# A fixed instruction order on every engine, 1024-column score steps, one-bank slots and a centred v, in a fused hash-attention and channel-mix kernel

## The chip, the cores and the metric

The kernel runs on one core of one Trainium2 chip. The metric is device time in microseconds of one execution. Most executions of one kernel agree closely; this kernel before the change spreads more than others (353 to 368 us in three runs). A run is called slow when it is over 1.5% above the fastest of the same kernel, and ratios below use fast runs alone. The profile of the kernel before fell in a slow run (366.5 us).

## The reference

Four batches, eight heads, 768 positions, head size 64. Each query attends only to keys in the same hash bucket; the result goes through a token-shifted channel mix.

```python
q_bits = (einsum('bhsd,dk->bhsk', q, proj) > 0)      # 6 bits; same for k
mask   = q_bucket[:, :, :, None] == k_bucket[:, :, None, :]
scores = where(mask, q @ k.T / 8, -1e9)
attn   = exp(scores - max);  attn /= attn.sum(-1) + 1e-9
x      = (attn @ v).transpose(0, 2, 1, 3).reshape(4, 768, 512)
x_prev = x shifted by one position, first row 0
xk = mu_k * x + (1 - mu_k) * x_prev                  # xr likewise with mu_r
out = sigmoid(xr @ w_r) * ((relu(xk @ w_k) ** 2) @ w_v)
```

A query whose bucket holds no key has to get the mean of v. The kernel does this with an epsilon weight on every key.

## The kernel before

It works on 16 pairs of heads. Four short names are used below. To "turn" is to transpose; q and k are first split into a rounded half (hi) and the remainder (lo). "Bit rows" are the six hash bits of each position, written by DMA as six more rows under q and k, so that the score matmul itself favours keys of the same bucket. "PV" is the product of the weights with v. A "mixed pair" is one beside which channel mix of an earlier batch runs. The parts that matter here:

```python
ps = ctx.enter_context(tc.tile_pool(name="ps", bufs=4, space=bass.MemoryType.PSUM))
# every use of PSUM takes one of these four slots of two banks, tag "s"

def mk_t(side):                  # split into hi and lo halves, turn by DMA
    ...                          # hi on POOL from pair 2 on, lo on VectorE
    nc.sync.dma_start_transpose(out=tr, in_=hl.rearrange("p c e -> p (c e)"))

def u_bits():                    # signs of the projections -> 6 bit rows under q and k
    bp = ps.tile([P, 2, 512], FP32, name=f"bp{n}", tag="s")
    ...                          # 16 matmuls, two VectorE passes
    nc.sync.dma_start(out=s["qk"[g // 2]][D:AUG, g % 2, :], in_=bt[G * g : G * g + NB, :])

def score_units(n):              # 12 units: 2 matmuls of 384 columns, one exp of 768
    ...
def pv_units(n):                 # epsilon: a matmul of eps_mat with the sum of v starts oo
    if ic == 0:
        hold["oo"] = ps.tile([P, 2, 512], FP32, name=f"oo{n}", tag="s")
        nc.tensor.matmul(hold["oo"][...], eps_mat, s["sv"]..., start=True, stop=False)
    ...                          # 72 matmuls of 65 columns into the slot; reciprocal; multiply

def k2_units(b):                 # relu on VectorE, square on POOL
    nc.vector.tensor_scalar(out=kr, in0=kp[:, :, 0:STRIP], scalar1=0.0, ..., op0=ALU.max)
    nc.gpsimd.tensor_tensor(out=k2, in0=kr, in1=kr, op=ALU.mult)

for n in range(NPAIRS):
    load(n + 3)
    ...
    weave(score_units(n + 1), front_units(n + 2), pv, moe.get(n, []))
```

The source order is not the order in which engines run: a scheduler may move an instruction ahead of others on its engine.

The softmax here doesn't subtract the row's maximum and nothing guards it: scores larger than these inputs give would overflow.

## Time and profile before

| | before |
|---|---|
| time, median of 3 runs | 358.08 us (353.14 to 367.58) |
| profiled execution | span 364.7 us, slow |
| first exp | 44.5 us |
| pairs 2 to 4, without channel mix | about 17 us each |
| end of the last exp to the end | 47.2 us (317.5 to 364.7) |

First the head of the profile page: the span, then busy time of each engine with its share. Below it are rows of the second part, 40 equal slices of the span (one is 9.1 us), with the busy share in tenths and the granted clock of TensorE in tenths of full speed.

```profile
span 364.7 us, 6121 instructions
PE 277.4 (76%) x2446; PEld 157.9 (43%) x2465; DVE 171.3 (47%) x275; ACT 176.1 (48%) x217; POOL 131.0 (36%) x187
...
PE   0020498396969698697979996969899989989795
...
ACT  1000197264746558275566683745567657710111
...
PEclk9999999556565699898999998978999999999989
DMA  7999789783735536456282560440616000011012
```

No engine is full on average. TensorE comes nearest and does next to nothing in the first four slices; after the eighth its row swings between 5 and 9. In slices 8 to 14 (63 to 126 us) the recorded clock is about half.

The waits view (engine, instruction, what it waited for, total us, times, longest):

```profile
ACT pt_242 L275 <- PE sc_0_0_243 L268: 42.2, 1, 42.2
...
PE bp_164 L213 <- DMA qt_157<-qhl_154: 19.9, 1, 19.9
...
PE sc_1_3_444 L268 <- DVE ob_462 L331: 6.0, 1, 6.0
```

The first says that no exp could start for 42 us. The second is why: the DMA transpose of q for pair 0 landed only at 19.9 us. The third is a score unit that waited 6 us for a PSUM slot that a normalisation had not yet read.

The stretch table (start and end in us, length, then busy us with instruction count for TensorE, its weight loads, VectorE, ScalarE and POOL, then granted clock, DMA share, GB/s):

```profile
75.00:92.00 17.00, 13.80 (x129) 8.30 (x127) 7.63 (x13) 10.50 (x13) 4.78 (x10) 0.60 0.66 170
...
285.00:300.00 15.00, 13.54 (x154) 8.51 (x152) 9.09 (x16) 9.96 (x13) 8.48 (x12) 1.00 0.02 4
```

The first is a pair without channel mix at half clock, the second one with mix at full clock. The chain of waits (start, length, what) leads in the tail through POOL's squares, one behind the other; TensorE has other matmuls beside most of them, and its own waits for squares come to 2.0 us there:

```profile
335.08 1.47 POOL k_3_0_3930 L388
336.55 1.43 POOL k_3_1_3943 L388
337.97 1.42 POOL k_3_2_3956 L388
```

### The profile page before, as it was taken

What the parts mean: (1) busy time and instruction counts of PE and PEld (TensorE: products, weight loads), DVE (VectorE), ACT (ScalarE), POOL (GpSimd) and SP (SyncE); (2) the same over time, 40 slices, a digit from 0 to 9 for tenths busy, and PEclk for the clock granted to TensorE, in tenths of its full rate; (3) what the DMA queues carried; (4) which work ended last, traced back from release to release, by engine and by line L of the source; (5) the groups of instructions that cost most, each with busy time, mean ns of one, the idle gap of its engine ahead of it and who ended that gap; (6) DMA issues with size and microseconds to landing.
All of it is one profiled execution on the core that took longest, in us unless ns stands there. A gap on an engine that the chain in (4) does not pass through costs nothing. (4 is left out here: it accounts for less than half of the span.)

```text
span 364.7 us, 6121 instructions
## 1 busy us (share of the span) xinstructions
PE 277.4 (76%) x2446; PEld 157.9 (43%) x2465; DVE 171.3 (47%) x275; ACT 176.1 (48%) x217; POOL 131.0 (36%) x187
## 2 busy tenths in 40 slices
PE   0020498396969698697979996969899989989795
PEld 0000245163636365363545552634455656555342
DVE  3321511636262566663545765633435665357422
ACT  1000197264746558275566683745567657710111
POOL 3643311522232356562323674622023642002900
PEclk9999999556565699898999998978999999999989
DMA  7999789783735536456282560440616000011012
GB/s 215 246 177 190 157 204 189 260 218 97 171 82 140 111 110 115 106 76 174 62 242 67 133 135 0 105 59 34 144 36 118 4 3 33 29 70 50 0 63 109
DMA packets 69788, 41.36 MB, mean 113 GB/s; under 512 B 51960, under 2 KB 66176, under 8 KB 69760
## 3 DMA queue, kind: packets, MB, share of 16 engines
q1 hardware_dynamic: 67632, 38.36, 44.1%
q0 software_dynamic: 2128, 2.62, 4.9%
q8 instruction: 19, 0.31, 0.4%
q14 instruction: 9, 0.07, 0.1%
HBM read 24.12 MB, written 6.29 MB: 83 GB/s over the span
## 5 line engine op out<-in xcount | busy, mean ns | idle before, releaser
L376 PEld LDWEIGHTS <-wk_sb 128*128 128x128 bf16 x256 | 25.3, 101 | 26.6 <-issue 13.0
L213 PEld LDWEIGHTS <-phi 128*32 128x32 f16 x128 | 4.3, 105 | 43.8 <-issue 36.9
L275 ACT ACTIVATE pt_242<-sc_0_0_243,exp_bias 128x768 bf16<-128x768 f32 x1 | 0.9, 902 | 42.2 <-PE sc_0_0_243 L268 42.2
L213 PE MATMUL bp_164<-qt_157,phi 128*32 128x384 f16 x4 | 1.0, 508 | 19.9 <-DMA qt_157<-qhl_154 19.9
L213 PE MATMUL bp_206<-qt_199,phi 128*32 128x384 f16 x4 | 1.0, 508 | 10.0 <-DMA qt_199<-qhl_196 10.0
L408 ACT ACTIVATE rs_0_4028<-vr_0_4023 128x512 f32<-128x512 f32 x1 | 0.6, 597 | 14.0 <-PE vr_0_4023 L400 14.0
L268 PEld LDWEIGHTS <-kt_162 70*128 70x128 f16 x24 | 3.3, 143 | 7.3 <-issue 4.1
L314 PEld LDWEIGHTS <-pt_694 128*128 128x128 bf16 x72 | 5.3, 137 | 2.4 <-issue 2.4
L314 PEld LDWEIGHTS <-pt_495 128*128 128x128 bf16 x72 | 5.2, 136 | 2.4 <-issue 2.4
L314 PEld LDWEIGHTS <-pt_242 128*128 128x128 bf16 x72 | 5.2, 134 | 2.4 <-issue 2.0
L314 PEld LDWEIGHTS <-pt_298 128*128 128x128 bf16 x72 | 5.1, 133 | 2.4 <-issue 2.4
L268 PEld LDWEIGHTS <-kt_204 70*128 70x128 f16 x24 | 2.4, 131 | 8.1 <-DVE ob_462 L331 6.4
L301 PEld LDWEIGHTS <-eps_mat 128*128 128x128 bf16 x32 | 3.4, 111 | 5.0 <-issue 3.4
L314 PE MATMUL oo_303<-va_188,pt_242 128*128 128x65 bf16 x72 | 5.5, 244 | 0.0
L314 PE MATMUL oo_897<-va_649,pt_694 128*128 128x65 bf16 x72 | 5.4, 246 | 0.0
L268 PE MATMUL sc_1_3_444<-qt_199,kt_204 70*128 70x384 f16 x2 | 0.8, 514 | 6.0 <-DVE ob_462 L331 6.0
L134 POOL TENSOR_SCALAR wv_sb<-wv_sb 128x2048 bf16<-128x2048 bf16 x2 | 3.9, 1948 | 4.0 <-DMA wv_sb<-in_moe_w_v_dram 4.0
L314 PE MATMUL oo_699<-va_452,pt_495 128*128 128x65 bf16 x72 | 5.3, 245 | 0.0
L314 PE MATMUL oo_500<-va_230,pt_298 128*128 128x65 bf16 x72 | 5.2, 241 | 0.0
L213 PE MATMUL bp_164<-kt_162,phi 128*32 128x384 f16 x4 | 1.1, 507 | 5.1 <-DMA kt_162<-khl_159 5.1
L213 PEld LDWEIGHTS <-plo 128*32 128x32 f16 x128 | 4.1, 109 | 1.5 <-issue 0.6
L240 POOL CAST va_3273<-vn_2807 128x768 bf16<-128x768 f32 x1 | 0.9, 896 | 10.8 <-PE oo_2835 L314 10.8
(1441 smaller groups left out, 996.5 us busy)
## 6 DMA issues: line engine op xcount, KB each, us to landing
wk_sb<-in_moe_w_k_dram POOLq DMA_DIRECT2D x2, 512.0 KB, 9.9
wv_sb<-in_moe_w_v_dram POOLq DMA_DIRECT2D x2, 512.0 KB, 12.4
wr_sb<-in_moe_w_r_dram POOLq DMA_DIRECT2D x1, 512.0 KB, 11.6
qn_134<-in_q_dram SPq DMA_DIRECT2D x1, 384.0 KB
kn_135<-in_k_dram SPq DMA_DIRECT2D x1, 384.0 KB
vn_136<-in_v_dram SPq DMA_DIRECT2D x1, 384.0 KB
qn_140<-in_q_dram SPq DMA_DIRECT2D x1, 384.0 KB
kn_141<-in_k_dram SPq DMA_DIRECT2D x1, 384.0 KB
```

Of the source, the lines that this page charges most:

```text
L134: nc.gpsimd.tensor_scalar(out=d, in0=d, scalar1=scale, scalar2=1.0, op0=ALU.mult, op1=ALU.mult)
L213: nc.tensor.matmul(bp[G * g : G * (g + 1), sp, 0:STRIP], (phi, plo)[w], s["qk"[g // 2]][:, g % 2, sp * STRIP : (sp + 1) * STRIP], start=(w ...
L240: nc.gpsimd.tensor_copy(va[:, :, :, 0:D], vn)
L268: nc.tensor.matmul(sc[:, sp, 0:STRIP], s["k"][0:AUG, j, jc * P : (jc + 1) * P], s["q"][0:AUG, j, sp * STRIP : (sp + 1) * STRIP], start=Tru ...
L275: nc.scalar.activation(pt[:, j, jc, :].rearrange("p (s q) -> p s q", s=2), sc[:, :, 0:STRIP], AF.Exp, bias=exp_bias, scale=EXP_SCALE,)
L301: nc.tensor.matmul(hold["oo"][:, j, 0 : NSC * W].rearrange("p (c w) -> p c w", c=NSC), eps_mat, s["sv"][:, j : j + 1, :].to_broadcast([P, ...
L314: nc.tensor.matmul(oo[:, j, ic * W : (ic + 1) * W], s["pt"][:, j, jc, ic * P : (ic + 1) * P], s["va"][:, j, jc, :], start=False, stop=(ic ...
L376: nc.tensor.matmul(kp[:, sp, 0:STRIP], wk_sb[:, dc, fc * P : (fc + 1) * P], mixed[b * NPB + dc][0][:, sp * STRIP : (sp + 1) * STRIP], star ...
L408: nc.scalar.activation(rs, vr[:, 1, :], AF.Tanh, scale=0.5)
```

## The change

The intent is to let TensorE run without gaps. Every engine gets a written order (a chain of dependencies without semaphores keeps each instruction behind the one before it in the source); each pair is nine steps of 1024 score columns with named side work at each step; the channel mix is dealt out evenly; PSUM is cut into two 2-bank slots for scores and four 1-bank slots for all else. Relu goes to ScalarE, squares and hi parts to VectorE. Pair 0 is turned by TensorE. The epsilon matmul is replaced: v has its mean taken off, the sum gets a plain epsilon, and the mean is added after the turn. Buffer counts change too (20 square buffers in place of 10, for strips half as long), and the loads are spread over the steps. The diff, cut to its core:

```diff
-    ps = ctx.enter_context(tc.tile_pool(name="ps", bufs=4, space=bass.MemoryType.PSUM))
+    sps = ctx.enter_context(tc.tile_pool(name="sps", bufs=2, space=bass.MemoryType.PSUM))
+    ops = ctx.enter_context(tc.tile_pool(name="ops", bufs=4, space=bass.MemoryType.PSUM))
+    def bank(name, shape=None, dtype=FP32):
+        return ops.tile(shape or [P, BANK], dtype, name=name, tag="o")
 ... (cut: loads, splits, turns)
+    def turn_by_pe(n, side):          # pair 0 only: 12 transposes, one copy out of PSUM
 ...
+    def v_mean(n):
+        nc.tensor.matmul(mp[:, 0:P], ones_mat, s["sv"], start=True, stop=True)
+        nc.tensor.matmul(mp[:, P : P + 1], s["sv"], ones_mat[:, 0:1], start=True, stop=True)
+        ...                           # va = v - mean, on POOL
 ...
-                nc.vector.tensor_scalar(out=kr, ..., op0=ALU.max)
-                nc.gpsimd.tensor_tensor(out=k2, in0=kr, in1=kr, op=ALU.mult)
+        nc.scalar.activation(kr, kp[:, 0:STRIP], AF.Relu, scale=0.5**0.5)
+        nc.vector.tensor_tensor(out=k2, in0=kr, in1=kr, op=ALU.mult)
 ...
+    def side_work(n, i):              # what goes beside score step i of pair n
+        if i == 1: pv_part(n - 1, head 1), pv_norm(n - 1, 1)
+        if i == 3: x_turn(n - 1)
+        if i in (6, 7): pv_part(n, head 0, half of it)
+        if i in (3, 4): bits_strip(n + 1, i - 3);   if i == 4: bits_place(n + 1)
+        if i == 0: split and DMA turn of q(n + 2);  if i == 2: the same of k(n + 2)
+        if i in (1, 5, 7): load q, k, v of pair n + 3
 ...
+    last = {}
+    for ins in list(nc.cur_bb.bb.instructions):
+        prev = last.get(ins.engine)
+        if prev is not None:
+            tc.add_manual_dep(ins, prev.name, NoSync ...)
+        last[ins.engine] = ins
```

## The prediction

> **What bounds the kernel now.** Three stretches, read from the timeline and the stretch table (busy time and granted clock by window); span 364.7 us.
>
> 1. Start, 0 to 43.6 us. The waits view has ScalarE idle 42.2 us until the first scores. The timeline shows why: four DMA transposes of q and k take until 39.7 us, the bit rows land about 43.6 us.
> 2. The 16 head pairs. Reciprocals of successive pairs (one per pair) stand at 67.3, 85.3, 102.2, 119.1 us: 17.2 us a pair while there is no channel mix. Two 384-column score matmuls then take 0.64 us instead of 0.33 us: TensorE has a half clock (granted 0.60 from 63 to 126 us), after a 6.0 us stall on a PSUM slot held for a DVE output ("sc_1_3 waits for ob", 6.0). From pair 4 to 15 the mean is 17.3 us (137.3 to 327.1 over 11). Undisturbed pairs take 14.3 to 15.3 us, disturbed ones 18 to 21, waiting for DMA bit rows (3.9 us in the chain) and DVE/PSUM slots.
> 3. Tail, 327 to 364.7 us: 32 us of matmuls plus gaps behind POOL squares at 1.47 us each (chain of waits, 335 to 346.6 us).
>
> TensorE's own need at full clock, from start-to-start times: scores 3.9, PV 72 x 33 ns = 2.4, bits 0.6, transposes and rest 0.5, and per batch 26 us of channel mix, 6.5 a pair: about 13.9 us a pair with mix, 7.4 without.
>
> **What the change does.**
> - Pair 0 is transposed on TensorE: first score near 20 us (estimate: load 4 us, two DVE splits of 1.5 us, two turns and evictions, bit strips, 5 us to place bits). Gain about 23 us.
> - Exp in 144 pieces of 1024, not 192 of 768. Start-to-start now is 0.79 us per 768; I estimate 1.06 per 1024, 9.5 us a pair: little gain by itself.
> - Relu goes from DVE (32 x 0.96 us) to ScalarE (64 x about 0.4 us); squares from POOL (32 x 1.47 us) to DVE (64 x about 0.3 us); POOL's hi parts (0.83 us) go to DVE. DVE becomes about 12 us a pair with mix, ScalarE 12: below TensorE.
> - Epsilon matmuls go, tiny mean matmuls come: near zero.
> - The order: no slot held for long, bits placed four steps ahead, mix spread evenly. Mixed pairs should run close to TensorE: 15 us instead of 17.3, 11 pairs, gain 25 us.
> - Pairs 0 to 3: ScalarE-bound at 9.5 us if TensorE is warm, 15 us if at half clock; early DMA (7 to 9 tenths busy in the first 90 us now) may delay transposes. I take 14 us.
> - Tail: the last batch's mix stays, but squares no longer gate it: about 38 us after the last exp, against 47 now.
>
> Sum: 20 + 4x14 + 14 + 11x15 + 38 + 3 = 296 us.
>
> The Trainium skill, "TensorE: Matmul & The Clock Gate", Part 1, says the half clock is the idle default and sustained activity releases it; the trace agrees (0.32 us per 384 columns at 44 us, 0.16 at 284 us).
>
> **Prediction: 296 us, 80% range 278 to 318.** Faster by over 2%: 0.96; within 2%: 0.03; slower: 0.01.
>
> **Signs.** First exp at 18 to 23 us; pair period 14 to 16 us in the mix; PE busy share over 85%; granted clock near 1.0 after 90 us; tail all TensorE.
>
> **What would make it wrong.** Early pairs still cold (plus 10 us), or DMA transposes late for the in-order TensorE queue (plus 10 to 20 us); DVE, in order and 80% loaded, gating PSUM banks; or early pairs at 10 us and a fully warm clock (minus 15).

## The result

| | before | after |
|---|---|---|
| median of 3 runs | 358.08 us | 292.83 us (291.74 to 294.45) |
| profiled span | 364.7 us (slow) | 289.9 us (fast) |
| first exp | 44.5 us | 24.0 us |
| pairs 0 to 4, first exp to first exp | 80.5 us | 73.6 us |
| pairs 5 to 14, mean of one | 17.8 us | 14.3 us |
| end of last exp to end | 47.2 us | 36.8 us |

The ratio is 0.824 (95% interval 0.808 to 0.840). A ratio is the mean time of one kernel's fast runs over that of the other's fast runs in the same rounds, so it is not quite the ratio of the medians. The left column comes from a slow run, so the differences of its lines add up to more than the fast runs differ by.

The same views of the kernel after. The head of the page and the slices (now 7.2 us each):

```profile
span 289.9 us, 6269 instructions
PE 250.1 (86%) x2489; PEld 146.0 (50%) x2489; DVE 203.5 (70%) x415; ACT 196.7 (68%) x234; POOL 83.6 (29%) x141
...
PE   0346919777679999999999999999999999999994
...
ACT  1015517894836999887879998777899978827420
...
PEclk9999999997965999999999999999999999999999
DMA  6207995598968894895975646878573001111022
```

From slice 13 (87 us) to the last but one the TensorE row is nines. This is not in itself proof of a full engine: the Trainium skill ("Trainium Kernel Development and Optimization", Performance Expectations) calls matmul busy time a bad metric for the distance to the roofline, because matmuls are pipelined. From 261.8 us on, eight channel-mix matmuls of 384 columns are recorded as 0.33 us long each, and start 0.16 us apart. The starts of successive matmuls are the better measure, and here they stand back to back.

The waits that answer to those shown of before:

```profile
PE qtp_145 L196 <- DVE qhl_142 L177: 9.8, 1, 9.8
...
ACT pt_242 L295 <- PE sc_0_243 L287: 7.3, 1, 7.3
...
PE sc_0_384 L287 <- DMA tr_215<-bt_278: 5.9, 1, 5.9
```

The long wait for a transpose is gone. A new one stands in the third line: the first scores of pair 1 wait 5.9 us for their bit rows. Two stretches, an early pair and a mixed one, in the same columns as before:

```profile
82.00:97.00 15.00, 15.00 (x130) 8.71 (x128) 11.16 (x19) 9.74 (x10) 7.24 (x11) 0.57 0.86 197
...
140.00:155.00 15.00, 15.00 (x159) 8.91 (x158) 12.81 (x25) 11.79 (x14) 5.22 (x11) 1.00 0.81 192
```

Pair 4 is still at half clock for most of its time. The mixed stretch is full on TensorE, at full clock, with VectorE at 12.8 of 15 us. The chain's last part is TensorE alone:

```profile
278.87 1.73 PE vp_3_4353 L409 x8
281.46 1.73 PE vp_4_4372 L409 x8
284.05 1.74 PE vp_5_4391 L409 x8
```

### The profile page after: what moved, and what is told of

The parts are those of the page before. It is cut to its first block, busy times and chain, and to the rows that moved or that the text cites. A ratio compares the mean times of both kernels' runs of the same rounds, so it can differ in the third digit from the quotient of the medians.

```text
span 289.9 us, 6269 instructions
## 1 busy us (share of the span) xinstructions
PE 250.1 (86%) x2489; PEld 146.0 (50%) x2489; DVE 203.5 (70%) x415; ACT 196.7 (68%) x234; POOL 83.6 (29%) x141
## 4 chain that ended last, share of the span: by engine, by line
PE 75%; DVE 8%; DMA 8%; SPq 3%; ACT 3%; issue 1%; ACTq 0%; DVEq 0%
SPq L239 3%; DMA proj_113<-in_proj_dram 2%; DMA tr_215<-bt_278 2%; DMA kn_520<-in_k_dram 1%; DMA tr_215<-khl_220 1%; ACT pt_785 L295 1%; ACT pt_383 L295 1%; PE oo_1_805 L306 1%; PE oo_1_1006 L306 1%; PE oo_1_403 L306 1%; PE oo_0_329 L306 1%; DMA tr_394<-bt_672 1%; PE vp_0_3757 L409 1%; PE vp_0_2716 L409 1%; PE vp_5_3211 L409 1%
## 5 line engine op out<-in xcount | busy, mean ns | idle before, releaser
L377 PEld LDWEIGHTS <-wk_sb 128*128 128x128 bf16 x256 | 23.5, 98 | 17.2 <-issue 2.6
L196 PE MATMUL qtp_145<-ident_h,qhl_142 128*128 128x128 f16 x12 | 1.5, 312 | 9.8 <-DVE qhl_142 L177 9.8
L217 PEld LDWEIGHTS <-phi 128*32 128x32 f16 x128 | 3.6, 95 | 12.1 <-issue 10.6
L205 ACT COPY tr_141<-ktp_162 128x1536 f16<-128x1536 f16 x1 | 1.4, 1439 | 11.5 <-PE ktp_162 L196 11.5
L287 PEld LDWEIGHTS <-tr_141 70*128 70x128 f16 x24 | 2.7, 132 | 8.4 <-DMA tr_141<-bt_184 4.4
L287 PEld LDWEIGHTS <-tr_215 70*128 70x128 f16 x24 | 2.3, 115 | 8.8 <-DMA tr_215<-bt_278 6.6
L287 PE MATMUL sc_0_384<-tr_215 70*128 70x256 f16 (+1 forms) x3 | 1.0, 484 | 5.9 <-DMA tr_215<-bt_278 5.9
L287 PEld LDWEIGHTS <-tr_595 70*128 70x128 f16 x24 | 2.6, 131 | 7.0 <-DMA tr_595<-bt_873 4.0
L196 PEld LDWEIGHTS <-qhl_142 128*128 128x128 f16 x12 | 1.2, 145 | 9.8 <-DVE qhl_142 L177 9.8
L295 ACT ACTIVATE pt_242<-sc_0_243,exp_bias 128x1024 bf16<-128x1024 f32 x1 | 1.1, 1113 | 7.3 <-PE sc_0_243 L287 7.3
L268 POOL TENSOR_TENSOR va_229<-vn_176,mean_227 128x384 bf16<-128x384 f32 x2 | 1.9, 994 | 11.8 <-DVE mu_sb L151 11.8
L306 PEld LDWEIGHTS <-pt_242 128*128 128x128 bf16 x72 | 4.5, 135 | 1.2 <-issue 1.1
L287 PEld LDWEIGHTS <-tr_394 70*128 70x128 f16 x24 | 2.1, 107 | 5.9 <-DMA tr_394<-bt_672 4.0
L295 ACT ACTIVATE pt_383<-sc_0_384,exp_bias 128x1024 bf16<-128x1024 f32 x1 | 1.1, 1113 | 5.9 <-PE sc_0_384 L287 5.9
L287 PE MATMUL sc_0_243<-tr_141 70*128 70x256 f16 (+1 forms) x3 | 1.0, 484 | 4.3 <-DMA tr_141<-bt_184 4.3
L306 PEld LDWEIGHTS <-pt_785 128*128 128x128 bf16 x72 | 3.6, 116 | 1.7 <-issue 1.4
L268 POOL TENSOR_TENSOR va_318<-vn_182,mean_316 128x384 bf16<-128x384 f32 x2 | 1.9, 996 | 7.9 <-DVE mean_316 L261 7.9
L287 PE MATMUL sc_0_987<-tr_595 70*128 70x256 f16 (+1 forms) x3 | 1.0, 485 | 3.6 <-DMA tr_595<-bt_873 3.6
L306 PEld LDWEIGHTS <-pt_584 128*128 128x128 bf16 x72 | 3.6, 116 | 0.7 <-issue 0.3
```

Source lines behind the costliest of these rows:

```text
L196: nc.tensor.transpose(tp[:, c // per, (c % per) * P : (c % per + 1) * P], st[n]["hl" + side][:, c, :], ident_h,)
L205: nc.scalar.copy(dst, tp[:, :, 0:S])
L217: nc.tensor.matmul(bp[G * g : G * (g + 1), 0:STRIP], (phi, plo)[w], rows(n, "qk"[g // 2])[:, g % 2, sp * STRIP : (sp + 1) * STRIP], start= ...
L268: nc.gpsimd.tensor_tensor(out=va[:, j, :, 0:D], in0=loaded[n, "v"][:, j], in1=mean[:, j * D : (j + 1) * D].unsqueeze(1).to_broadcast([P, N ...
L287: nc.tensor.matmul(sc[:, at - i * UNIT : upto - i * UNIT], rows(n, "k")[0:AUG, j, jc * P : (jc + 1) * P], rows(n, "q")[0:AUG, j, q0 : q0 + ...
L295: nc.scalar.activation(s["pt"][:, i * UNIT : end], sc, AF.Exp, bias=exp_bias, scale=EXP_SCALE)
```

## The experiments

Two theories were set against each other first. Theory O: the written order carries the mixed pairs. Theory E: the move of relu and squares does. All results below were correct, and each ratio is to the kernel before in the same rounds. Periods of pairs are read from the first exp of each pair in the profile of that run.

### free_order: the changed kernel without the chain

```diff
-    last = {}
-    for ins in list(nc.cur_bb.bb.instructions):
-        ... (the whole loop)
```

> The changed kernel without the chain that fixes the order on each engine; every operation is the same. Theory O (the written order is what carries the mixed pairs): the scheduler pulls loads and transposes ahead of the bit rows again (its queue shows four loads and four transposes before the first bit rows), so the first exp comes later than 24.0 us, pairs wait for bit rows, mixed pairs go from 14.2 to 15.5-17 us; 310 to 330 us in all. Theory E (the move of relu and squares carries it): mixed pairs stay within 14.2 to 14.7 us and only the start is lost, 293 to 303 us.

Measured: 322.25 us (319.59 to 324.12), ratio 0.906; the profile is of a fast run. The first exp comes at 38.0 us, and pairs 5 to 14 take 16.8 us each instead of 14.3. So the order is worth about 29 us (322.25 less 292.83), with every operation the same. Theory O holds. Its expected detail was only partly right: late bit rows held the start, but in the mixed pairs something else did. The waits of 104 to 284 us, first the longest of TensorE and then the longest of VectorE for a DMA:

```profile
PE ot L335 <- DVE ob L324: 16.3, 7, 3.3
...
DVE qhl L171 <- DMA tr<-qhl: 15.6, 7, 4.6
```

TensorE's turn of the result waits for the normalised product on VectorE, seven times and 16.3 us in all, and no matmul there waits for bit rows. The timeline of this run at 139 us (start, length, engine, operation, idle time before it and what ended it):

```profile
139.38 0.56 DVE L171 TENSOR_SCALAR qhl<-qn 128x768 f16<-128x768 f32 x1 [4.57 <-DMA tr<-qhl]
...
141.32 0.16 DVE L320 TENSOR_SCALAR rc<-oo 128x6 f32<-128x6 f32 x1
...
142.70 0.56 DVE L171 TENSOR_SCALAR khl<-kn 128x768 f16<-128x768 f32 x1 [1.22 <-DMA tr<-khl]
143.18 0.18 DVE L323 RECIPROCAL rc<-rc 128x6 f32<-128x6 f32 x1
143.30 0.96 DVE L177 SCALAR_TENSOR_TENSOR khl<-kn,khl 128x768 f16<-128x768 f32 x1
144.17 0.55 DVE L324 TENSOR_TENSOR ob<-oo,rc 128x384 bf16<-128x384 f32 x1
...
144.78 0.55 PE L335 MATMUL ot<-ident_b,ob 128*128 128x128 bf16 x6 [3.34 <-DVE ob L324]
```

The scheduler has put the splits of a pair far ahead in front of the normalisation. Each split waits for its buffer, which is free only when a DMA transpose has read it: 4.57 us, then 1.22. The reciprocal and the product behind it, which need nothing from the DMA, wait too, and TensorE waits 3.34 us for the product. The Trainium skill ("TensorE: Matmul & The Clock Gate", Part 1, on engine queue depths) says that VectorE's queue is strictly first in, first out; the trace agrees, since a ready normalisation stood 1.2 us behind a split that was not. In the written order (the kernel after) the same instructions stand the other way round:

```profile
114.68 0.17 DVE L320 TENSOR_SCALAR rc_1_1570<-oo_1_1533 128x6 f32<-128x6 f32 x1 [0.35 <-PE oo_1_1533 L306]
114.88 0.19 DVE L323 RECIPROCAL rc_1_1570<-rc_1_1570 128x6 f32<-128x6 f32 x1
115.10 0.56 DVE L324 TENSOR_TENSOR ob_1456<-oo_1_1533,rc_1_1570 128x384 bf16<-128x384 f32 x1
115.58 0.55 DVE L171 TENSOR_SCALAR khl_1581<-kn_1387 128x768 f16<-128x768 f32 x1
```

The 29 us are a balance. Against the kernel after, free_order loses 14.0 us at the start and 25.0 us from pair 5 to the last exp, has the same tail (36.8 us), and gains 7.7 us in pairs 0 to 4 (65.9 us against 73.6). And it is still some 34 us faster than the kernel before. So a little over half of the whole gain doesn't need the written order; the experiments below undo other parts one by one, on the changed kernel with the order kept, and none of them says what carries these 34 us.

### before_ordered: the kernel before with the chain

```diff
+    last = {}
+    for ins in list(nc.cur_bb.bb.instructions):
+        ... (the same loop as in the change)
```

> The kernel before with the same chain added, so each engine runs in the order of its source; no operation changed. Theory O in its strong form (any fixed order helps): 320 to 340 us. Theory O in its weak form (the order has to be a good one; this source issues bit rows just before they are used and holds PSUM slots long): no gain, 350 to 380 us. Theory E: no gain, 350 to 370 us.

Measured: 420.13 us (418.86 to 423.91), ratio 1.183, slower by more than expected; against the fast runs of the kernel before in the same rounds (357.63 and 353.69) it loses about 65 us. Pairs 5 to 14 take 22.6 us each. The longest waits of TensorE's matmuls from 120 to 365 us:

```profile
PE ot L342 <- DVE ob L331: 17.1, 10, 1.9
PE bp L213 <- DMA kt<-khl: 14.8, 7, 2.5
```

A fixed order is no gain in itself: this source was written for a scheduler, and in its order TensorE stands before a turn until the normalisation is done, and before the bit rows' matmuls until k has been turned. Theory O holds only in its weak form: what helps is a good order, kept.

### old_mix_engines: relu back on VectorE, squares back on POOL

```diff
-        nc.scalar.activation(kr, kp[:, 0:STRIP], AF.Relu, scale=0.5**0.5)
-        nc.vector.tensor_tensor(out=k2, in0=kr, in1=kr, op=ALU.mult)
+        nc.vector.tensor_scalar(out=kr, in0=kp[:, 0:STRIP], scalar1=0.0, scalar2=0.5**0.5, op0=ALU.max, op1=ALU.mult)
+        nc.gpsimd.tensor_tensor(out=k2, in0=kr, in1=kr, op=ALU.mult)
```

> The changed kernel with relu back on VectorE (64 of about 0.56 us) and squares back on POOL (64 of about 0.8 us), order kept. Theory O: TensorE stays gap-free since four one-bank slots cover the longer chain; VectorE gets busier by about 1 us a mixed pair, mixed pairs 14.2 to 14.8 us, 292 to 302 us. Theory E: mixed pairs go back to 15.5-17 us, 310 us or more.

Measured: 296.71 us (294.36 to 298.65), ratio 0.834. Pairs 5 to 14 take 14.75 us each against 14.3. By the medians the move of engines is worth about 4 us, but the intervals of the two ratios overlap (0.821 to 0.847 against 0.808 to 0.840), so this is not clear of noise. (The hi parts stay on VectorE in this run.) Theory E falls. The tail takes 37.2 us against 36.8, though the squares are back on POOL.

### before_new_mix: the kernel before with the new relu and squares

```diff
-                nc.vector.tensor_scalar(out=kr, in0=kp[:, :, 0:STRIP], scalar1=0.0, ..., op0=ALU.max)
-                nc.gpsimd.tensor_tensor(out=k2, in0=kr, in1=kr, op=ALU.mult)
+                nc.scalar.activation(kr, kp[:, :, 0:STRIP], AF.Relu)
+                nc.vector.tensor_tensor(out=k2, in0=kr, in1=kr, op=ALU.mult)
```

> The kernel before with relu on ScalarE (32 of about 0.9 us in place of 0.96 us on VectorE) and squares on VectorE (32 of about 0.55 us in place of 1.47 us on POOL); order and slots as before. Theory O: the waits for bit rows and slots stay, only the tail shortens by some 5 us (the chain of POOL squares from 335 to 346.6 us goes): 345 to 360 us. Theory E: 330 us or less.

Measured: 355.64 us (348.62 to 358.49), ratio 0.986 with an interval from 0.952 to 1.020. Two of the four runs are slow; the fast ones took 348.62 and 352.8 us. So a small gain is possible and none is shown. Seen from this side too, the moves alone are not the gain. Its profile and that of the kernel before are both slow runs; there the tail takes 43.9 us against 47.2.

### dma_start: pair 0 turned by the DMA

```diff
     for side in "qk":
         hi_part(0, side)
         lo_part(0, side)
-        turn_by_pe(0, side)
+        turn_by_dma(0, side)
```

> The changed kernel with pair 0 turned by the DMA instead of TensorE; nothing else differs. If the TensorE turn carries the gain of the start (first exp 24.0 us against 44.5), the first exp comes 6 to 12 us later than 24.0[...] and the total rises by the same, to 299-306 us. Rival: the start was won by the order of the load queue, not by the turn; then first exp within 3 us of 24.0 and total 291-296 us.

Measured: 289.76 us (287.32 to 291.15), ratio 0.799. The first expectation was wrong and the rival holds, with a total slightly below its band: undoing the turn on TensorE costs nothing, and its runs even lie a little below those of the changed kernel (in other rounds). Its timeline:

```profile
7.75 1.55 SPq L187 DMA_TRANSPOSE tr<-qhl  x1
...
9.35 1.81 SPq L187 DMA_TRANSPOSE tr<-khl  x1
11.21 0.89 SPq L101 DMA_DIRECT2D vn<-in_v_dram  x1
11.72 0.50 PE L217 MATMUL bp<-tr,phi 128*32 128x384 f16 x2 [11.72 <-DMA tr<-qhl]
```

The transposes of pair 0 now stand in the load queue in front of the loads of v and of pair 1, and q's is there 4.0 us after its issue; the first exp comes at 21.0 us, 3 us earlier than in the changed kernel. In the kernel before, the same transposes stood behind nine loads of 384 KB and were waited for until 19.9 and 25.5 us. In free_order pair 0 is turned by TensorE, but its bit rows are issued only at 32.0 us, behind four transposes of later pairs, and the first exp comes at 38.0 us. So the start was won by the order of the queue, not by the engine that turns.

### eps_matmuls: the epsilon matmul in place of the mean

```diff
+            nc.tensor.matmul(s["oo", j][:, 0 : NSC * W]..., ones_mat,   # filled with EPS
+                s["sv"][:, j : j + 1, :].to_broadcast([P, NSC, W]), start=True, stop=False)
 ... (va is a plain copy of v; sv has 65 columns)
-        nc.vector.tensor_scalar(out=rc, in0=oo[:, :, D:W], scalar1=EPS, scalar2=None, op0=ALU.add)
-        nc.vector.reciprocal(rc, rc)
+        nc.vector.reciprocal(rc, oo[:, :, D:W])
 ... (v_mean and the addition after the turn go)
```

> The changed kernel with the epsilon weight as it was: two matmuls of 390 columns with the sum of v, no mean taken off or given back. TensorE gets 2 x 0.16 us more and 0.1 us less a pair at full clock, 16 pairs: about +3.5 us if all lies on TensorE's path; VectorE loses about 0.5 us and POOL about 1.5 us a pair, which returns something in the early pairs, where VectorE gates. My theory: near zero, 291 to 297 us. Rival (the mean is a real part of the gain): 300 us or more.

Measured: 294.37 us (292.91 to 295.49), ratio 0.814. Near zero, as expected: pairs 5 to 14 take 14.5 us instead of 14.3, and pairs 0 to 4 together 71.6 us instead of 73.6 (one profile each).

### steps_768: twelve steps of 768 columns

```diff
-    STEPS = 2 * NSC * S // UNIT
+    STEPS = 2 * NSC
 ... (a unit is again 2 matmuls of 384 columns and an exp of 768)
-        sides = [side_work(n, i) for i in range(STEPS)]
+        for i in range(9):
+            sides[(i + 1) * 4 // 3 - 1] = side_work(n, i)
```

> The changed kernel with 12 steps of 768 score columns a pair in place of 9 of 1024, the side work at the matching places. ScalarE: 192 exps 0.79 us apart = 9.5 us a pair, against 9 of about 1.01 us = 9.1. Theory: mixed pairs are held by TensorE (14.2 us), so the size of the step is worth nothing there and up to 0.4 us a pair in the early ones: 291 to 297 us. Rival (larger exps are what frees the pipe): 302 us or more.

Measured: 298.32 us (293.15 to 300.73), ratio 0.815. Two of the four runs are slow and pull the median 1 us above the expected band; the fast ones, 293.15 and 296.56 us, lie in it. Pairs 5 to 14 take the same 14.3 us; the early pairs take 78.3 us together instead of 73.6. So the step size is worth nothing in the mix. Whether the difference in the early pairs is the step or where the side work fell is not settled.

### slots2: two one-bank slots in place of four

```diff
-    ops = ctx.enter_context(tc.tile_pool(name="ops", bufs=4, space=bass.MemoryType.PSUM))
+    ops = ctx.enter_context(tc.tile_pool(name="ops", bufs=2, space=bass.MemoryType.PSUM))
```

> The changed kernel with two one-bank slots for everything but the scores in place of four, order kept. The change says one-bank slots for all other work; if more slots are part of why TensorE has no gaps, mixed pairs rise from 14.2 us to 17 us or more (each relu, turn and normalisation is then waited for, about 0.6 to 1 us each, some 8 a pair), 330 us or more. If the order alone carries it: under 305 us.

Measured: 315.29 us (313.17 to 316.09), ratio 0.871, between the two bands. Pairs 5 to 14 take 16.3 us each, in the same order. The waits of TensorE's matmuls from 110 to 250 us in this run (there are none at all of them in the changed kernel in that stretch):

```profile
PE kp L377 <- DVE ob L324: 5.0, 5, 1.2
...
PE kp L377 <- DVE xt L339: 2.4, 3, 0.8
```

A channel-mix unit waits until the normalisation or the copy after the turn has read its bank. The order needs enough slots to be kept without waiting; four do, two cost 22 us. The two sums are not to be added, since each was measured with the other part in place; no run has the free order with two slots.

### dma_bits, dma_loads, dma_both: what holds pairs 0 to 4

In the changed kernel and in dma_start these five pairs take 73.6 and 75.1 us, though a pair without mix needs about 9 us of ScalarE (nine exps 1.0 us apart) and an estimated 7.4 us of TensorE at full clock. VectorE is the busiest in the changed kernel: 8.8, 11.6 and 10.6 us in pairs 1 to 3, which took 11.9, 12.4 and 14.8. Three runs on dma_start tried two reasons alone and together.

```diff
 dma_bits:
-            if i in (3, 4):   bits_strip(nxt, i - 3);   place at 4
+            first = 3 if n == 0 else 1
+            if i in (first, first + 1):   bits_strip(nxt, i - first);   place at first + 1
-            if i == 0:  split and turn q(far);   if i == 2:  k(far)
+            the same, but at 4 and 5 for n == 0
 dma_loads:
-            if i in (1, 5, 7):   load q, k, v of n + 3
+            if i in (1, 2, 7):
 dma_both: both edits
```

> dma_start with the bit rows of the next pair made and placed at steps 1 and 2 in place of 3 and 4 (in pair 0 they stay at 3 and 4, but go ahead of pair 2's splits on VectorE). Open: why pairs 0 to 4 of dma_start take 15 us (19.4, 11.9, 18.0, 13.9, 11.8), with 4 to 8 us waits for bit rows at their ends. Theory B (bits are placed too close to their use): those waits go, pairs 0 to 4 take 11 to 13 us, total 276 to 283 us. Theory L (the load of k comes late and holds VectorE ahead of the bits): the wait moves into the pair and little is gained, 286 to 292 us. Theory D (the DMA engines are saturated): no change either.

> dma_start with the load of k three pairs ahead issued at step 2 in place of 5, so in front of the bit rows in the queue and not behind them. Theory L: the 2 us waits of VectorE for k go, pairs 1 to 4 come down by 1 to 3 us each, total 281 to 286 us. Theory B: the bit rows, now behind a load of 384 KB, land later still, total 289 to 295 us. Theory D: no change, 288 to 291 us.

> Both edits at once. Theory B or L or both: pairs 0 to 4 near 11 to 12 us each, that is 10 to 15 us less than dma_start: 274 to 280 us. Theory D: 286 us or more.

Measured: 289.24 (287.42 to 290.12), 289.10 (288.50 to 297.28) and 287.81 us (285.42 to 289.47); ratios 0.809, 0.809 and 0.805. Pairs 0 to 4 took 70.7, 72.6 and 71.9 us. The waits for bit rows went (from 16.8 us in dma_start to 3.6 in dma_both), and something else took their place. The chain of dma_both in pair 1 (start, length, what):

```profile
33.73 8.84 DMA tr<-khl
42.60 0.82 PE bp L217 x6
43.43 0.97 PE sc L287 x3
```

The transpose of k for pair 2 takes 8.8 us from issue to landing, and pair 1 takes 20 us. Theories B and L fall as the whole cause: the edits take the waits for bit rows away and the time stays. dma_bits and dma_both also moved pair 2's splits later in pair 0 and pair 1's need for the result earlier, so the new wait in pair 1 may be of their own making.

### pe_early: pairs 2 to 5 turned on TensorE too

```diff
-                w.append((0, lambda: turn_by_dma(far, "q")))
+                turn = turn_by_pe if far <= 5 else turn_by_dma
+                w.append((0, lambda: turn(far, "q")))           # and for k; on top of dma_both
```

> dma_both with pairs 2 to 5 turned on TensorE (24 transposes a pair, evicted by one VectorE and one ScalarE copy) in place of the DMA; pairs 0 and 1 and from 6 on by the DMA. In dma_both the waits for bit rows have turned into a wait of pair 1 for the DMA transposes of pair 2 (8.8 us from issue to landing), and pairs 0 to 4 still take 72 us. Theory D (the crowded DMA engines hold the early pairs): 8 transposes fewer there let pair 1 fall from 20 to 13 us or less, pairs 0 to 4 to 62 to 66 us, total 277 to 282 us. Rival (the early pairs are held by the copies on VectorE and ScalarE or by the half clock of TensorE): pairs 0 to 4 stay at 70 us or more, total 286 to 292 us.

Measured: 310.50 us (305.51 to 312.08), ratio 0.867, worse than either band; the three fast runs took 305.51 to 309.83. The DMA engines' share fell to 0.22 to 0.41 between 36 and 90 us (0.76 to 1.06 in dma_both), yet pairs 0 to 4 took 89.0 us, and the first three about 20 each. In the fixed order TensorE now stands before each turn until VectorE has split the half (waits of 20 to 120 us):

```profile
PE ktp L196 <- DVE khl L177: 10.3, 4, 2.6
```

So a busy DMA is not enough to explain the early pairs either. This run does not refute a part for the DMA, as it put a new wait where it took the old one away. What holds pairs 0 to 4 stays open: each edit moved the wait (bit rows, transposes, splits), and large parts of these pairs ran at half clock in every run (PV matmuls 54 to 55 ns apart, against 32 to 33 at full clock). Half clock alone is not enough either: pair 2 of the changed kernel ran at the full rate and took 12.4 us. The shortest time for the five is that of free_order, 65.9 us (10.9, 12.8, 9.5, 17.2 and 15.5), so the written order may itself cost something here. But there the pairs start 14 us later, with more loads done, and no run separates the two.

## Why the prediction was right, and where it was not

The predicted time, 296 us, is 1.1% above the measured 292.83. The sum, term by term (measured from the profile of the kernel after, in first exps; 24.0 + 58.6 + 15.1 + 155.5 + 36.8 = 290.0, the span is 289.9):

| term | predicted us | measured us |
|---|---|---|
| start | 20 (first score) | 22.9 (first score), 24.0 (first exp) |
| pairs 0 to 3 | 56 | 58.6 |
| pair 4 | 14 | 15.1 |
| pairs 5 to 15 | 165 | 155.5 (97.6 to the end of the last exp at 253.1) |
| tail | 38, plus 3 of slack | 36.8 |

- **The mixed pairs.** Right in mechanism: slots held briefly, even work, and TensorE near its own need. The estimate of 13.9 us for that need was good; the 1.1 us of slack that I allowed on top was too much, since it measured 14.3. Two experiments bear the mechanism out: the same operations without the order take 16.8 us, with the order and two slots 16.3. Even mix by itself was not tested.
- **The start.** The size was about right and the reason was wrong. The step that failed is "Pair 0 is transposed on TensorE: first score near 20 us ... Gain about 23 us". With pair 0 turned by the DMA again the first exp comes at 21.0 us. What gains is that nothing stands in the queue in front of pair 0. That the forecast came near is luck to this extent. The sign "18 to 23 us" was just missed at 24.0.
- **Pairs 0 to 3.** The 14 us was a compromise between 9.5 (ScalarE) and 15 (half clock). It measured 14.6, with two reasons mixed: half clock, and waits for bit rows of up to 5.9 us, which the prediction had listed only as a risk with transposes in mind. The experiments did not settle which one leads, so that 14.6 came near to the compromise is partly luck.
- **The engine moves.** Predicted to leave VectorE and ScalarE at about 12 us a mixed pair, below TensorE. In the stretch from 110.9 to 125 us of the kernel after they were busy 12.95 and 12.21 of 14.1 us. VectorE came nearer to its limit than foreseen. One reason that the timeline suggests is POOL's work on v:

```profile
106.85 0.36 DVE L387 TENSOR_TENSOR k_0_7_0_1396<-kr_7_0_1394 128x384 bf16<-128x384 bf16 x1
107.23 1.06 DVE L387 TENSOR_TENSOR k_0_0_1_1405<-kr_0_1_1403 128x384 bf16<-128x384 bf16 x1
```

  and on POOL, in the same view:

```profile
106.98 2.17 POOL L268 TENSOR_TENSOR va_1383<-vn_978,mean_1381 128x384 bf16<-128x384 f32 x2 [3.09 <-DVE mean_1381 L261]
```

  (The first fence is the timeline of VectorE in the kernel after.) Squares of the same size take 0.36 us and then 1.06 us while POOL takes the mean off v. The Trainium skill ("SBUF — State Buffer", the shared port pair) says that VectorE with two SBUF inputs and a POOL operation that reads SBUF lock each other out for a whole instruction; the two lines agree with it. So does the rest of the trace: of the 64 squares, six start while POOL is at work for at least 0.2 us more, and these take 1.05 to 1.86 us; the other 58 take 0.35 to 0.36. That is some 5 us in all, so it explains a small part of VectorE's load. That the mean costs VectorE time in this way is read from the trace and was not tested by itself; without the mean (eps_matmuls) the total is no lower.
- **The mean of v and the step of 1024.** "Near zero" and "little gain by itself" held: 294.37 and 298.32 us (fast runs of the latter 293.15 and 296.56) with either undone.
- **The tail.** 36.8 us against the forecast 38, now TensorE end to end (0.2 us of waits). The size was right, but the step "squares no longer gate it" carries little of it. In the kernel before, TensorE waited 2.0 us for squares after the last exp, and moving them there shortens the tail by 3.3 us (before_new_mix, two slow runs); in the changed kernel the tail is 37.2 us even with the squares back on POOL. The rest of the 10.4 us has another source: less is left to do after the last exp, 36 PV matmuls and 93 of gate and value product against 74 and 104. No run isolates it.
- **The clock.** The prediction leaned on the Trainium skill ("TensorE: Matmul & The Clock Gate", Part 1) for the half clock as the idle state. The trace agrees: a 384-column matmul starts 0.32 us after the one before it at 44 us in the kernel before, and 0.16 us at 284 us. The agreement is about the two rates. What releases the clock this does not show: from 44 to 62 us of the kernel before, TensorE was busy by the profile for all of 18.0 us and kept the half rate (PV matmuls 54 to 55 ns apart). The sign "near 1.0 after 90 us" was met from 97 us on.

The lowest median is that of dma_both, at 287.81 us (ratio 0.805 against 0.824 of the change, in other rounds): the change without the turn on TensorE, with bit rows and the load of k earlier. It is some 2% below the changed kernel by the medians; the intervals of the ratios overlap, so it is not shown to be better. dma_start has the lowest ratio, 0.799; the four dma_ runs cannot be told apart.

## What to carry to other kernels

When a scheduler is free to hoist work, look in each in-order queue, VectorE's and the load queue's, for an instruction that waits on a DMA and stands in front of one that is ready and urgent; fixing the order was worth 29 us here with no operation changed, and fixing a bad order cost about 65. Give a fixed order enough PSUM slots to be kept without waits (two fewer cost 22 us). And undo each part of a change before crediting it: the part that looked like the gain of the start turned out to be worth nothing, and the squares' move gave the tail 0.4 us.

## What the Trainium skill lacked or had wrong

- "TensorE: Matmul & The Clock Gate", Part 1, gives the lengths of the busy and idle windows, but not how busy is busy. In the kernel before, the recorded clock averaged 0.59 from 63 to 126 us; in a 17 us pair of that stretch (75 to 92 us) TensorE was busy for 13.8 us by the profile; and from 44 to 62 us it kept the half rate though busy for all of 18.0 us.
- The same page warns that clock events in a trace can be unreliable, and a run here shows it: the page of dma_both records a clock of 1.00 for 55 to 70 us, where score steps of 1024 columns took 0.97 us; at 71.6 us such a step took 0.54. The two main profiles have it too: 1.00 is recorded for 44 to 62 us of the kernel before and 24 to 49 us of the kernel after, where PV matmuls started 54 to 55 ns apart. So in these profiles the PEclk row alone does not show where the half clock ends; the starts of matmuls do.
- "DMA: Bandwidth & Descriptors" has no time from issue to landing of a DMA transpose of 384 KB with other traffic in front of it. Here it was 4.0 us at the head of the queue (dma_start, 7.75 to 11.72 us), 5.75 us in mid-kernel (free_order) and 8.8 us in a crowded start (dma_both).
- No page says what a scheduler that hoists instructions does to an in-order engine. Here it cost 29 us net of 322 (free_order).
